# Merging K^T V stretches of two batches, moving the transfers that feed them, and splitting the last copy of an attention and MLP kernel

## The chip, the cores and the metric

The kernel runs on one core of a Trainium2 chip. The metric is the device time of one execution in microseconds (us). A profile's span is some 1.8 us shorter than the time. Executions of one kernel spread by 1 to 1.5 us around 284, and each is marked fast or slow by its time and granted TensorE clock.

## The reference

For 8 batches with 8 heads, 576 positions and 64 dimensions:

```python
kv  = np.einsum('bhsd,bhse->bhde', k, v)
out = np.einsum('bhsd,bhde->bhse', q, kv)
rms = np.sqrt(np.mean(out * out, axis=-1, keepdims=True) + 1e-06)
x   = (out / rms * g_norm)      # heads joined: 4608 rows of 512
h   = x @ w_in                  # 2048 wide
g   = np.where(h > 0, h, np.exp(np.minimum(h, 0)) - 1)
y   = g @ w_out                 # 512 wide
```

## The kernel before

The kernel works through nine groups of 512 rows: one for each batch's first 512 positions, and a ninth for the last 64 positions of all batches. Group T interleaves eight steps of the first product (w_in) of group T with pieces of the second product (w_out) of group T - 1. The attention of group T + 1 is put in between, and batch T + 2 is fetched. The parts that the change touches:

```python
def kv_single(T, kv_ps, u, ls=(0, 1)):      # 36 matmuls of 64x64 for each u
    for j in range(RK):
        for l in ls:
            for s in range(2):
                ...
                nc.tensor.matmul(kv_ps[...], lhsT=bf["k", T][...], rhs=bf["v", T][...], ...)

def fetch(b):
    if b < B:
        fetch_packed_q(b)
        packed_kv(b)
        for name in "kv":
            fetch_packed_kv(name, b)
        unpack_q(b, Q)
    ...

# in group(T, ...), at = attention(T + 1), ahead = attention(T + 2):
    for i in range(8):
        rest = mm1(T, i, ...)                # 8 matmuls of w_in, ScalarE's exp
        if at and i == 3:
            at["se"](...)                    # 32 score matmuls, need kv_sb of T + 1
        for piece in second.get(i, ()):
            mm2(T - 1, *piece)               # 8 matmuls of w_out
        ...
        rest()                               # VectorE: gT
        if at and i == 0:
            at["kv"]()                       # 72 matmuls of 64x64, one copy to kv_sb
        if at and i > 5:
            at[f"xg{i - 6}"]()               # VectorE: scaling of a half of x

# in the loop over groups:
    at["landed"]()                           # gpsimd waits until q's transpose landed
    fetch(T + 2)
    ...
    group(T, ...)
    ahead["qd"]()                            # q's transposing transfer, from SyncE
```

Of the kernel before, what the change touches and what calls it, by code (L numbers as in the profile page):

```python
# [8 lines left out]
FP32 = mybir.dt.float32  # L9
# [7 lines left out]
def kernel(  # L17
# [13 lines left out]
    nc = tc.nc  # L31
    P = 128

    B, H, S, D = q.shape
    DM = H * D
# [7 lines left out]
    NT = B + 1  # L43
# [52 lines left out]
    def fetch_packed_q(b):  # L96

        t = packed.tile([P, H, J, D], BF16, name="q_pk", tag="q")
        raw["q", b] = t
        in_ = q[b].rearrange("(h s) r d -> s h r d", s=2)[:, :, 0:G, :].rearrange(  # L100
            "s h (p j) d -> p s h (j d)", j=J
        )
        for s in range(2):
            nc.gpsimd.dma_start(  # L104
                out=t[:, 4 * s : 4 * s + 4].rearrange("p h j d -> p h (j d)"), in_=in_[:, s]
            )

    def packed_kv(b):
        for name, pool in (("k", packed), ("v", qkvp)):
            t = pool.tile([P, 4, RK, D], BF16, name=f"{name}_pk", tag=name)  # L110
            raw[name, b] = t
            bf[name, b] = t.rearrange("p h j d -> p j h d")

    def fetch_packed_kv(name, b, hs=slice(0, 4)):
        in_ = (k if name == "k" else v)[b].rearrange("h r d -> (h r d)").rearrange(
            "(h p x) -> p h x", h=4, p=P
        )
        nc.gpsimd.dma_start(  # L118
            out=raw[name, b].rearrange("p h j d -> p h (j d)")[:, hs], in_=in_[:, hs]
        )  # L120
# [3 lines left out]
    def after(ap):  # L124
        nc.gpsimd.tensor_copy(out=gate, in_=ap)  # L125

    def unpack_q(b, eng):
        t = raw.pop(("q", b))
        bf["q", b] = qkvp.tile([P, J, H, D], BF16, name="q_bf", tag="q")
        for j in range(J):  # L130
            if j == J - 1:
                after(bf["v", b][0:1, 0, 0, 0:1])
            copy_on(eng, bf["q", b][:, j], t[:, :, j])
# [12 lines left out]
    def copy_on(eng, out_, in_):  # L146
        if eng is nc.scalar:
            nc.scalar.copy(out_, in_)
        else:
            eng.tensor_copy(out=out_, in_=in_)  # L150
# [6 lines left out]
    def cast_q(b, eng):  # L157
        sv = q_tile(b)
        for j in range(J):
            copy_on(eng, bf["q", b][:, j], sv[:, j])  # L160
# [3 lines left out]
    def at_tile(dtype):  # L164
        full = ps_at.tile([P, 1024], FP32, name="at", tag="at")
        return full if dtype == FP32 else full.bitcast(BF16)

    def kv_single(T, kv_ps, u, ls=(0, 1)):
# [4 lines that stand above are left out]
                    rows = slice(s * 64, s * 64 + 64)  # L173
                    nc.tensor.matmul(  # L174
                        kv_ps[l * 64 : l * 64 + 64, s, u * 64 : u * 64 + 64],
                        lhsT=bf["k", T][rows, j, 2 * u + l, :],
                        rhs=bf["v", T][rows, j, 2 * u + l, :],
                        start=(j == 0),
                        stop=(j == RK - 1),
                    )  # L180
# [59 lines left out]
    def attention(T):  # L240
        st = {}
# [109 lines left out]
        def kv_out(us):  # L351
            nc.scalar.copy(
                kv_sb[:, T].rearrange("p (s u) e -> p s u e", s=2)[:, :, us],
                st["kv"][:, :, 0:P].rearrange("p s (u e) -> p s u e", u=2)[:, :, us],
            )

        def kv_u(u):
            def product():
                st["kv"] = at_tile(FP32).rearrange("p (s x) -> p s x", s=2)
                kv_single(T, st["kv"], u)  # L360
                kv_out(slice(u, u + 1))

            return product
# [61 lines left out]

            return turn

        pieces = {"kv": kv_all, "q": q_t, "qd": q_dma, "se": se}
        pieces["landed"] = lambda: after(st["at"])
        for h in range(2):  # L430
            pieces[f"kvu{h}"] = kv_u(h)
# [122 lines left out]
    for u in range(2):  # L554
        nc.sync.dma_start(
            out=q_raw0[:, u].rearrange("p (h x) -> p h x", h=4),
            in_=q[0, 4 * u : 4 * u + 4, 0:G, :].rearrange("h (p j) d -> p h (j d)", j=J),
# [24 lines left out]
    for s in range(2):  # L582
# [5 lines left out]
        out=g_row,  # L588
        in_=bass.AP(tensor=g_norm.tensor, offset=g_norm.offset, ap=[[1, 1], [0, 2], [1, 64]]),
# [34 lines left out]
    def turned(n):  # L624
# [7 lines left out]
        out=qT0.rearrange("p (s u) t -> p u s t", u=2)[:, 0], in_=qt_ps  # L632
# [134 lines left out]
    at, ahead = attention(1), attention(2)  # L767
    for i in range(3, 8):
        mm1(0, i, relu=i in (3, 5, 7), home={5: "m2", 6: "at"}.get(i, "m1"))()
    nc.gpsimd.tensor_copy(  # L770
        out=kv_sb[:, 0].rearrange("p (s u) e -> p u s e", s=2), in_=kv0
# [8 lines left out]
    both = ps_m1.tile([P, 2, G], FP32, name="o_ps", tag="mm1")  # L780
# [40 lines left out]

    def fetch(b):
        if b < B:
            fetch_packed_q(b)
            packed_kv(b)
            for name in "kv":
                fetch_packed_kv(name, b)
            unpack_q(b, Q)
        else:
            fetch_q(B)  # L830
            cast_q(B, Q)

    def group(T, at, lead, second, relu=()):

        for piece in lead:
            mm2(T - 1, *piece)
        if T == 2:
            for i in range(8):
                n = i // 2 - 1
                early = [at[f"sum{n}"], at[f"inv{n}"]] if i in (2, 4) else ()  # L840
                rest = mm1(T, i, relu=i in relu, between=early)
                for piece in second.get(i, ()):
                    mm2(T - 1, *piece)
                if i in (2, 4):
                    at[f"mul{n}"]()
                rest()
                if i in (2, 4):
                    at[f"xd{n}"]()
                if i == 0:
                    at["kv"]()  # L850
                if i in (1, 3):
                    at["se"]({i // 2: None})
                    at[f"sq{i // 2}"]()
                if i in (5, 6):
                    at[f"xg{i - 5}"]()
            return
        for i in range(8):
            between = [at["sq1"], at["sum0"], at["inv0"], at["sum1"]] if at and i == 4 else ()
            rest = mm1(T, i, relu=i in relu, between=between)
            if at and i == 3:  # L860
                at["se"]({0: None, 1: [ps_m2.tile([P, DM], FP32, name="se_ps", tag="mm2") for _ in range(2)]})
                at["sq0"]()
            for piece in second.get(i, ()):
                mm2(T - 1, *piece)
            if at and i == 4:
                at["inv1"]()
                for n in range(2):
                    at[f"mul{n}"]()
                    at[f"xd{n}"]()
            rest()  # L870
            if at and i == 0:
                at["kv"]()
            if at and i > 5:
                at[f"xg{i - 6}"]()

    ahead["landed"]()
    fetch(3)
    at, ahead = ahead, attention(3)
    ahead["qd"]()
    for i in range(8):  # L880
# [20 lines left out]
    for T in range(2, NT):  # L901
        at = ahead if T + 1 < NT else None
        if T + 2 < NT:
            at["landed"]()
            fetch(T + 2)
            ahead = attention(T + 2)
        if T == 2:
            lead, pieces, steps = [], [(2 + i // 4, 4 * (i % 4), 4 * (i % 4) + 4) for i in range(2, 8)], range(1, 7)
        elif T < B:
            lead, pieces, steps = halves[:1], halves[1:], (0, 1, 2, 4, 5, 6, 7)  # L910
        else:
            lead, pieces, steps = halves[:1], halves[1:], range(7)
        second = {i: [piece] for i, piece in zip(steps, pieces)}
        group(T, at, lead, second, {2: (1, 2, 4, 5), B: ()}.get(T, (4, 5)))
        if T + 2 < NT:
            ahead["qd"]()
    rows = out.rearrange("(i l s) f -> l s i f", l=2, s=S)
    pieces = [(j, slice(0, DM)) for j in range(J - 1)]
    pieces += [(J - 1, slice(0, DM // 2)), (J - 1, slice(DM // 2, DM))]
    for j, cols in pieces:  # L920
        n = cols.stop - cols.start
        ps = ps_m2.tile([P, DM], FP32, name="o_ps", tag="mm2")[:, 0:n]
        for f in range(FC):
            nc.tensor.matmul(  # L924
                ps,
                lhsT=gT[B][:, f, j * P : j * P + P],
                rhs=w_out_sb[:, f, cols],
                start=(f == 0),
                stop=(f == FC - 1),
            )  # L930
        sb = outp.tile([P, DM], FP32, name="o_last", tag="o_last", bufs=5)[:, 0:n]
        nc.scalar.copy(sb, ps)  # L932
        for l, eng in enumerate((nc.sync, nc.scalar)):
            eng.dma_start(out=rows[l, G:S, j, cols], in_=sb[l * 64 : l * 64 + 64, :])

# [29 lines left out]
```

## Time and profile before

| | before |
|---|---|
| time, median of the first 3 runs | 283.71 us (283.44 to 284.33) |
| span of the profiled run | 282.0 us |
| TensorE busy | 276.0 us, 98% |
| VectorE, ScalarE, gpsimd busy | 57%, 55%, 20% |
| one K^T V stretch in the chain | 0.71 us, and 0.10 on the matmuls behind it |
| last copy | 0.37 us |

In the chain of waits, a line is a start, a duration and what the time went to. In the timeline, square brackets give how long the engine was idle before and what ended that. The lines themselves stand in the prediction.

### The profile page before, as it was taken

To read this page: it belongs to the slowest core of one execution; us is meant where nothing else is said; L and a number is where in the kernel's file an instruction comes from. 1 tells how busy PE (TensorE), PEld (TensorE's weight loads), DVE (VectorE), ACT (ScalarE), POOL (GpSimd) and SP (SyncE) were. 2 spreads that over 40 slices of the span, in tenths; PEclk is the share of its full clock that TensorE was granted. 3 is DMA by queue.
4 is the path that set the end of the run, shared out by engine and by line. 5 is a ranking of instruction groups with operands and counts; after the bars stand their busy time and mean duration, and the time that the engine had idled before them with its cause. 6 is when DMAs were issued, how large, how long until landed. Compare 5 with 4: busy or idle time off the path is not lost.

```text
span 282.0 us, 5163 instructions
## 1 busy us (share of the span) xinstructions
PE 276.0 (98%) x2134; PEld 129.8 (46%) x2134; DVE 159.8 (57%) x232; ACT 153.8 (55%) x221; POOL 56.2 (20%) x98
## 2 busy tenths in 40 slices
PE   7899999999999999999999999999999999999994
PEld 3444544445444444444444444444444444444444
DVE  2559453888388546843693469445854586444400
ACT  2679546666487438533863377337923692333311
POOL 7854422143421341004110421012000000000000
PEclk9999999999999999999999999999999999999999
DMA  7999999697796696359935795455236123010122
GB/s 196 199 200 202 208 201 191 179 170 128 178 177 114 157 157 156 74 149 121 198 78 148 95 211 73 130 114 148 55 94 76 77 38 112 0 77 0 74 76 74
DMA packets 57579, 35.98 MB, mean 128 GB/s; under 512 B 32852, under 2 KB 55124, under 8 KB 57556
## 3 DMA queue, kind: packets, MB, share of 16 engines
q0 software_dynamic: 21808, 17.30, 41.2%
q1 hardware_dynamic: 35348, 17.83, 24.7%
q10 hardware_dynamic: 400, 0.52, 0.6%
q8 instruction: 16, 0.26, 0.4%
q14 instruction: 7, 0.06, 0.1%
HBM read 36.70 MB, written 9.44 MB: 164 GB/s over the span
## 4 chain that ended last, share of the span: by engine, by line
PE 94%; DMA 2%; ACT 1%; DVE 0%; issue 0%; POOL 0%; POOLq 0%
PE h_ps L467 42%; PE o_ps L514 39%; PE o_ps L924 5%; DMA v_pk<-in_v_dram 2%; PE at L174 2%; PE at L467 1%; PE bank L684 1%; PE at L201 1%; PE h_ps L684 1%; PE se_ps L201 1%; ACT r L669 0%; ACT r L672 0%; PE at L185 0%; ACT sq L663 0%; PE se_ps L413 0%
## 5 line engine op out<-in xcount | busy, mean ns | idle before, releaser
L467 PE MATMUL h_ps<-xT,w_in_sb 128*128 128x512 bf16 x536 | 125.7, 379 | 0.0
L514 PE MATMUL o_ps<-w_out_sb,gT 128*128 128x512 bf16 x512 | 120.5, 379 | 0.0
L479 ACT ACTIVATE elu_e<-h_ps 128x1024 bf16<-128x1024 f32 (+1 forms) x71 | 70.0, 995 | 80.1 <-PE h_ps L467 78.5
L467 PEld LDWEIGHTS <-w_in_sb 128*128 128x128 bf16 x552 | 52.5, 98 | 63.3 <-DVE xT L333 1.7
L514 PEld LDWEIGHTS <-gT 128*128 128x128 bf16 x512 | 49.4, 98 | 58.4
L490 DVE TENSOR_SCALAR elu_e<-elu_e 128x1024 bf16<-128x1024 bf16 (+1 forms) x75 | 31.9, 425 | 73.4 <-ACT elu_e L479 73.4
L498 DVE TENSOR_TENSOR gT<-elu_e,h_ps 128x1024 bf16<-128x1024 bf16 (+1 forms) x51 | 60.1, 1179 | 5.3
L527 ACT COPY o_sb<-o_ps 128x512 f32<-128x512 f32 x32 | 18.6, 586 | 15.5 <-PE o_ps L514 15.5
L218 DVE TENSOR_REDUCE ss<-sq 128x16 f32<-128x1024 bf16 x16 | 19.4, 1218 | 11.1 <-ACT sq L213 10.4
L485 ACT ACTIVATE elu_h<-h_ps 128x1024 bf16<-128x1024 f32 (+1 forms) x20 | 19.5, 990 | 0.0
L150 POOL COPY q_bf<-q_pk 128x512 bf16<-128x512 bf16 x24 | 14.4, 629 | 24.3 <-DMA q_pk<-in_q_dram 24.3
L498 DVE TENSOR_TENSOR gT<-elu_e,elu_h 128x1024 bf16<-128x1024 bf16 x20 | 14.2, 709 | 2.5 <-ACT elu_h L485 1.0
L924 PE MATMUL o_ps<-w_out_sb,gT 128*128 128x512 bf16 (+1 forms) x80 | 14.1, 337 | 0.0
L125 POOL COPY gate<-qT 1x1 bf16<-1x1 bf16 x6 | 1.1, 181 | 58.4 <-DMA qT<-q_bf 58.4
L104 POOL DMA_DIRECT2D q_pk<-in_q_dram x14 | 10.6, 758 | 4.5 <-issue 1.5
L229 DVE TENSOR_TENSOR xs<-at,ss 128x512 bf16<-128x512 f32 x16 | 10.2, 682 | 1.2 <-ACT ss L225 1.2
L924 PEld LDWEIGHTS <-gT 128*128 128x128 bf16 x80 | 7.8, 98 | 6.4 <-DVE gT L498 0.4
L213 ACT ACTIVATE sq<-at 128x1024 bf16<-128x1024 f32 x9 | 9.4, 1043 | 1.6 <-PE at L201 1.0
L118 POOL DMA_DIRECT2D k_pk<-in_k_dram x12 | 8.3, 690 | 3.9 <-DMA w_in_sb<-in_moe_w_in_dram 2.4
L118 POOL DMA_DIRECT2D v_pk<-in_v_dram x12 | 8.2, 683 | 3.2 <-DMA w_out_sb<-in_moe_w_out_dram 1.8
L932 ACT COPY o_last<-o_ps 128x512 f32<-128x512 f32 (+1 forms) x5 | 2.5, 500 | 10.8 <-PE o_ps L924 10.8
L174 PEld LDWEIGHTS <-k_pk 64*64 64x64 bf16 x576 | 6.4, 107 | 4.3 <-issue 4.0
(79 smaller groups left out, 140.7 us busy)
## 6 DMA issues: line engine op xcount, KB each, us to landing
out_dram<-o_sb SPq DMA_DIRECT2D x16, 512.0 KB, 3.3
q_pk<-in_q_dram POOLq DMA_DIRECT2D x14, 256.0 KB, 5.7
k_pk<-in_k_dram POOLq DMA_DIRECT2D x6, 576.0 KB, 8.3
v_pk<-in_v_dram POOLq DMA_DIRECT2D x6, 576.0 KB, 11.6
w_in_sb<-in_moe_w_in_dram POOLq DMA_DIRECT2D x5, 256.0 KB, 7.4
st_q<-in_q_dram SPq DMA_DIRECT2D x2, 512.0 KB, 4.7
w_out_sb<-in_moe_w_out_dram POOLq DMA_DIRECT2D x2, 512.0 KB, 13.9
w_out_sb<-in_moe_w_out_dram POOLq DMA_DIRECT2D x4, 256.0 KB, 12.0
```

What stands on the lines that cost most here:

```text
L118: nc.gpsimd.dma_start(out=raw[name, b].rearrange("p h j d -> p h (j d)")[:, hs], in_=in_[:, hs])
L150: eng.tensor_copy(out=out_, in_=in_)
L174: nc.tensor.matmul(kv_ps[l * 64 : l * 64 + 64, s, u * 64 : u * 64 + 64], lhsT=bf["k", T][rows, j, 2 * u + l, :], rhs=bf["v", T][rows, j, 2 ...
L218: nc.vector.reduce_sum(out=ss, in_=sq.rearrange("p c (h e) -> p (c h) e", h=H), axis=AX.X)
L467: nc.tensor.matmul(h_ps[a][:, cs], lhsT=w_in_sb[:, c, f * P : f * P + P], rhs=x(c, cs), start=(c == 0), stop=(c == KC - 1),)
L479: nc.scalar.activation(e[:, lo:hi, :], ps, AF.Exp)
L485: nc.scalar.activation(h[:, lo:hi, :], ps, AF.Relu)
L490: nc.vector.tensor_scalar(out=e[:, lo:hi, :], in0=e[:, lo:hi, :], scalar1=1.0, scalar2=1.0, op0=ALU.min, op1=ALU.subtract,)
L498: nc.vector.tensor_tensor(out=gT[T][:, 2 * i + lo : 2 * i + hi, :], in0=e[:, lo:hi, :], in1=h, op=ALU.add if relu else ALU.max,)
L514: nc.tensor.matmul(o_ps[T, j], lhsT=gT[T][:, f, j * P : j * P + P], rhs=w_out_sb[:, f, :], start=(f == 0), stop=(f == FC - 1),)
L527: nc.scalar.copy(o_sb[T][:, j % 2, :], o_ps.pop((T, j)))
L924: nc.tensor.matmul(ps, lhsT=gT[B][:, f, j * P : j * P + P], rhs=w_out_sb[:, f, cols], start=(f == 0), stop=(f == FC - 1),)
```

## The change

The intent is to pay the entry into and exit from 64x64 tiles twice less: K^T V of batches 4 and 5 runs as one stretch in group 3, that of 6 and 7 in group 5, each in one PSUM tile. Batches 5 and 7 are then wanted a group earlier. So q's transposing transfer is issued right behind x's, which opens the next fetch earlier, and k and v go ahead of q for these two. Last, the final 128x256 copy is divided between ScalarE and VectorE. The core of the diff (the two-line helper `kv_in` and its names are cut):

```diff
     def fetch(b):
         if b < B:
-            fetch_packed_q(b)
             packed_kv(b)
+            if b < 5 or b % 2 == 0:
+                fetch_packed_q(b)
             for name in "kv":
                 fetch_packed_kv(name, b)
+            if b >= 5 and b % 2:
+                fetch_packed_q(b)
...
                 if i in (5, 6):
                     at[f"xg{i - 5}"]()
+                if i == 5:
+                    ahead["qd"]()
             return
...
-            if at and i == 0:
-                at["kv"]()
+            if i == 2 and T % 2 and T + 2 < B:
+                both = at_tile(FP32).rearrange("p (s x) -> p s x", s=2)
+                for n, a in enumerate((at, ahead)):
+                    a["kvin"](both[:, :, n * P : n * P + P])
+                for a in (at, ahead):
+                    a["kvout"]()
...
+            if i == 5 and T + 2 < B:
+                ahead["qd"]()
...
-        if T + 2 < NT:
+        if T + 2 == B:
             ahead["qd"]()
...
-        nc.scalar.copy(sb, ps)
+        if cols.stop == DM and n < DM:
+            nc.scalar.copy(sb[:, 0 : n // 2], ps[:, 0 : n // 2])
+            nc.vector.tensor_copy(out=sb[:, n // 2 : n], in_=ps[:, n // 2 : n])
+        else:
+            nc.scalar.copy(sb, ps)
```

More of the change, by code (lines that the diff above doesn't have):

```diff
@@ L355, in kv_out, with kv_in @@
             )
+        def kv_in(home):
+            st["kv"] = home
+            for u in range(2):
+                kv_single(T, home, u)
         def kv_u(u):
@@ L426, in x_u @@
             return turn
-        pieces = {"kv": kv_all, "q": q_t, "qd": q_dma, "se": se}
+        pieces = {"kv": kv_all, "kvin": kv_in, "kvout": lambda: kv_out(slice(0, 2)), "q": q_t, "qd": q_dma, "se": se}
         pieces["landed"] = lambda: after(st["at"])
```

## The prediction

> **What bounds the kernel now.** I read the page's busy times first, then the chain that ended last, then the timeline of the engines around one K^T V stretch and of the queues that feed it.
>
> ```profile
> PE 276.0 (98%) x2134; PEld 129.8 (46%) x2134; DVE 159.8 (57%) x232; ACT 153.8 (55%) x221; POOL 56.2 (20%) x98
> ...
> PE 94%; DMA 2%; ACT 1%; DVE 0%; issue 0%; POOL 0%; POOLq 0%
> ```
>
> TensorE is busy for 276.0 of 282.0 us and makes 94% of the chain; the other engines have over 40% idle. The rest of the chain is the first load (6.10 us) and the first batch's normalization, neither of which the diff touches. So time can be won in two ways only: fewer TensorE microseconds between the first 20 us and the end, or a shorter tail after the last matmul. It can be lost wherever TensorE is made to wait. The chain around the K^T V of batch 4, and the end (start us, us, what):
>
> ```profile
> 95.31 1.73 PE o_ps L514 x8
> 97.03 0.71 PE at L174 x72
> 97.74 1.83 PE h_ps L467 x8
> 99.57 1.73 PE o_ps L514 x8
> ...
> 264.43 13.92 PE o_ps L924 x80
> 278.35 0.02 issue
> 278.37 0.37 ACT o_last L932
> ```
>
> Eight 512-column matmuls take 1.73 us everywhere (0.216 us each) except behind a 64x64 stretch, where the same eight take 1.83. One K^T V therefore costs TensorE 0.71 + 0.10 = 0.81 us. The third view is what the gpsimd queue and SyncE do about this time (start us, us, engine, line, operation, tiles, idle before and its releaser):
>
> ```profile
> 87.35 1.23 SPq L326 DMA_TRANSPOSE xT<-xs  x1
> 90.83 0.34 SPq L536 DMA_DIRECT2D out_dram<-o_sb  x1
> 91.27 2.62 SPq L256 DMA_TRANSPOSE qT<-q_bf  x1
> 95.81 0.18 POOL L125 COPY gate<-qT 1x1 bf16<-1x1 bf16 x1 [7.57 <-DMA qT<-q_bf]
> 96.27 0.87 POOL L104 DMA_DIRECT2D q_pk<-in_q_dram  x1 [0.27 <-issue]
> 99.05 0.76 POOL L118 DMA_DIRECT2D v_pk<-in_v_dram  x1
> 103.74 1.92 POOL L150 COPY q_bf<-q_pk 128x512 bf16<-128x512 bf16 x3 [3.93 <-DMA q_pk<-in_q_dram]
> 110.17 0.18 POOL L125 COPY gate<-v_pk 1x1 bf16<-1x1 bf16 x1 [4.50 <-DMA v_pk<-in_v_dram]
> ```
>
> Batch 5 is fetched only after batch 4's transposed q has landed (95.81), q before k and v, and its v is there at 110.17. TensorE does not mind: it uses them in the group after this one.
>
> **What the Trainium skill says.** "TensorEngine Tiling (Array Packing)", Key Properties: "Changing tiling mode (not just tile) drains the TensorE". The trace agrees in size: an isolated stretch of 36 64x64 matmuls in batch 1 costs 0.41 us and makes the four matmuls after it 0.97 instead of 0.86, so 0.52; 72 cost 0.81. Thus 36 more cost 0.29, and 0.81 - 2 x 0.29 = 0.23 us is fixed, whatever the number. "DMA: Bandwidth & Descriptors", Anatomy of one DMA, says that a transfer has a fixed part of about 2 us, mostly completion, beside its bytes; here the first bytes after the issue at 96.27 flow only from about 98 (6 GB/s in 96 to 98, 136 in the next two). "PSUM — Partial Sum Buffer", on bank collisions, says that ScalarE and VectorE must not read the same bank and 32-partition quadrant at once. The kernel before has no such pair side by side in its trace, so nothing here confirms it, but the new last copy is exactly that pair.
>
> **The change part by part.** First, the merged stretches. K^T V of 4, 5, 6 and 7 are four stretches now, 4 x 0.81 = 3.24 us. In two stretches of 144 matmuls each costs 0.23 + 4 x 0.29 = 1.39, so 2.78 together. All of it is on TensorE's path: minus 0.46 us. The number of matmuls and the data do not change.
>
> Second, the copies out. Two CASTs of 128x256 at 0.37 us each follow the double stretch (0.74), and the score product of the next step needs their result and their PSUM tile. Between lie the eight w_in matmuls of step 3 with 1.83 us, and ScalarE's exp and output copy of step 2 are over by then. About 1 us is left: no cost.
>
> Third, the supply. In the group of T = 3 TensorE now wants batch 5 after step 2. Step 3 starts at 104.75 in the trace of before; batch 4's stretch is no longer ahead of it, so the double stretch starts at 104.75 - 0.81 = 103.94 and batch 5's half at 104.65. With the old order (landed 110.17) TensorE would stand for 5.5 us, so the two moves of transfers have to pay for this. q's transposing transfer goes right behind x's: the issue of x's second half ends at 87.35 + 1.23 = 88.58, q_bf is complete at 88.24, so q is issued at 88.6 instead of 91.27 and lands 4.54 later as now, at 93.1. The first fetch follows 0.46 later, at 93.6, and it is k. In the trace v landed 13.9 us after the first issue (96.27 to 110.17). Of that, q's 0.52 MB took about 4.1 us (136 and 110 GB/s from 98 to 102), which now comes behind: 9.8 us, so v lands at 103.4 at the latest. The output store of 0.5 MB that shared the engines from 105.4 does not fall into the new window, which should give back up to 2 us: my estimate is 101.5 to 103.4. Slack 1.2 to 3.1 us, so no wait. For batch 7 in the group T = 5 the q transfer moves more, from 151.19 to about 145.3 (x's issues end at 145.56, the schedule is then 0.23 ahead), so k is issued at 150.3, v is there by 160.1 at the latest, and TensorE wants it at 162.7: slack 2.6. q itself comes later for 5 and 7, but its unpacked form is needed only at about 117 and 175, over 5 us after it can be ready.
>
> Fourth, x behind which q now stands. x's transfers are still issued first. The scaling of x's second half starts at 122.01 because VectorE works on gT until then, while x landed at about 119.6 (3.2 after its issue ended at 116.4): q's packets behind it have 2 us to disturb before it shows.
>
> Fifth, the last copy. ScalarE's 372 ns for 128x256 becomes 128x128 on ScalarE (a 128x128 copy from PSUM has 258 ns in this trace) and 128x128 on VectorE (289 ns for a 64x128 copy from PSUM). Side by side: 0.37 - 0.29 = 0.08 us won. But both halves lie in one bank, and if the program is ordered so that they do not collide, VectorE waits for ScalarE: 0.26 + 0.03 + 0.29 = 0.58, that is 0.21 us lost. I think the ordered form likelier, 60 to 40, which makes plus 0.09 on average.
>
> Sum: 283.71 - 0.46 + 0.09 = 283.34, so **283.3 us**.
>
> **The rivals.** (a) TensorE waits for v of batch 5. For it: this batch gains only 2.7 us by the moved transpose, and my slack has 1.2 us at its low end. Against it: it needs q's removal from the front to be worth under 3 us. A late v by 1 us would make 284.3; with nothing gained by the order of k, v and q (landing at 93.6 + 13.9 = 107.5) a wait of 2.9 us, 286.2. I give a visible wait 15%. (b) The fixed part is not a cost of the switch but of the first accumulation of each batch, and merging saves nothing: about 283.7 to 283.8. Against it: the 0.10 us on the matmuls after a stretch is the same for stretches of 36 and 72 and for score stretches, so at least 2 x 0.10 = 0.2 us should go. (c) The last copy runs side by side: 283.2. (d) VectorE or the gpsimd queue becomes a bound because copies of q move under VectorE's work. Against it: VectorE is at 57%, and the same number of copies only shifts by 3 to 5 us; at most some tenths, in one group.
>
> **Range and chances.** The runs of before spread from 283.44 to 284.33, so a median moves by some 0.3 by itself. (b) and (c) span 283.2 to 283.8, (a) has a tail to 286. Range 282.7 to 284.0. A change of 2% is 5.7 us: nothing on the gaining side has that size (all K^T V stretches of these batches together are 3.2), and on the losing side only a supply failure in both groups. Faster 0.005, same 0.985, slower 0.01.
>
> **What would show it.** Right: two stretches of 144 64x64 matmuls of 1.3 us in the chain, no VectorE or DMA share in the chain beyond the first load, TensorE busy at about 275.6, gate on qT near 93 instead of 95.81, v of batch 5 seen before 104.6. Wrong: a piece "DMA v_pk" in the middle of the chain, or idle TensorE ahead of the second half of a double stretch (a); a double stretch of over 1.55 us (b). The last copy: two 128x128 copies that overlap (c), or a VectorE copy whose idle time ends with ScalarE's. The prediction as a whole falls if the time leaves 282.7 to 284.0, most likely upwards by a wait for v.

## The result, and the profile after

The changed kernel took 284.45 us as the median of six runs. One of them was a slow run of 481.57 us (clock 0.56); the five fast ones spread from 283.81 to 284.83, with a median of 284.31. The kernel before had 283.85 in six runs. A ratio here is the mean time of one kernel's fast runs over that of the kernel before in the same rounds, so not quite the ratio of the medians quoted. It is 1.0011, with a 95% interval of 0.999 to 1.0033. Two later sets of runs gave 1.0007 and 1.0013. The change is worth nothing, or costs about 0.3 us; it was expected to win 0.4.

The first profile fell in the slow run, and a second one too (738.01 us, with matmuls of 0.83 us in place of 0.38). Each was the first of that kernel's six executions, and nothing is read from their times. A third profile is fast, with a span of 282.5 us. Its page shows busy times and the chain by engine (30 of 2134 matmul records are missing, so its busy TensorE is a little low, and its chain has false gaps of 0.05 us and short detours):

```profile
PE 272.9 (97%) x2104; PEld 129.2 (46%) x2134; DVE 160.4 (57%) x233; ACT 153.5 (54%) x221; POOL 56.0 (20%) x98
...
PE 91%; ACT 3%; DMA 2%; DVE 2%; issue 1%; POOL 0%; POOLq 0%
```

TensorE is still the bound. The chain around both double stretches and at the end:

```profile
102.25 1.73 PE o_ps L519 x8
103.98 1.33 PE at L174 x144
105.31 1.83 PE h_ps L472 x8
...
162.14 1.31 PE at L174 x144
163.45 1.83 PE h_ps L472 x8
165.28 0.34 PE at L201 x16
165.68 0.46 issue
166.14 0.35 PE se_ps L201 x12
...
278.72 0.27 ACT o_last L949
279.00 0.02 issue
279.02 0.29 DVE o_last L950
```

Each double stretch takes 1.31 to 1.33 us, with 0.10 behind it, just as worked out. But in group 5, two steps after the stretch, TensorE stands for 0.46 us in the middle of its score matmuls, and the profile knows of nothing that it waits for ("issue"). At the end the two halves of the last copy come one after the other. The gpsimd queue shows the supply of batch 5:

```profile
92.74 0.18 POOL L125 COPY gate<-qT 1x1 bf16<-1x1 bf16 x1 [5.19 <-DMA qT<-q_bf]
93.26 0.75 POOL L118 DMA_DIRECT2D k_pk<-in_k_dram  x1 [0.34 <-issue]
94.56 0.75 POOL L118 DMA_DIRECT2D v_pk<-in_v_dram  x1 [0.56 <-issue]
```

The gate opens at 92.74 (predicted 93.1). By the packet records the last bytes of v leave at 101.5, and its landing is signalled at 102.16, 1.8 us before TensorE begins the stretch. There is no wait for data.

To see where the time went I cut each profile at the first w_in matmul of groups 4, 5, 6 and 7. "Steady" runs from the first w_in matmul in the steady loop's line to the end of the last matmul, and "tail" from there to the end of the span. All numbers are us from timelines of fast profiles; names are those of the experiments below.

| kernel | starts at | until group 4 | group 4 | group 5 | group 6 | steady | tail |
|---|---|---|---|---|---|---|---|
| before | 19.68 | 102.86 | 29.14 | 29.14 | 29.14 | 258.65 | 3.62 |
| changed (again2) | 19.83 | 103.38 | 28.40 | 30.37 | 28.33 | 258.86 | 3.83 |
| one_copy | 20.00 | 103.61 | 28.56 | 30.26 | 28.32 | 259.14 | 3.61 |
| split_only | 20.16 | 102.77 | 29.14 | 29.14 | 29.14 | 258.56 | 3.83 |
| moves_only | 19.95 | 102.92 | 29.33 | 29.14 | 29.13 | 258.90 | 3.61 |
| phase64 | 20.23 | 103.47 | 28.44 | 29.74 | 28.33 | 258.36 | 3.62 |
| phase118 | 19.79 | 104.85 | 28.33 | 30.15 | 28.33 | 260.03 | 3.61 |
| early_scale | 19.79 | 103.37 | 28.30 | 30.34 | 28.30 | 258.67 | 3.60 |
| phase60 | 20.40 | 103.57 | 28.41 | 29.74 | 28.33 | 258.42 | 3.62 |
| best | 20.30 | 103.46 | 28.31 | 29.72 | 28.31 | 258.13 | 3.61 |

The start differs by half a microsecond between kernels with the same program there (before and split_only), because the first transfers do. Hence the steady part is compared, and the runs' totals beside it. In the changed kernel, groups 4 and 6 lose their single stretch (0.74 and 0.81 us less). The part before group 4 gains 0.52 (group 3 by itself 0.6) and group 5 gains 1.23, where the prediction had 0.58 each. So 0.65 us too much sit in group 5, and 0.21 us in the tail.

### The profile page after: what moved, and what is told of

Read it like the earlier page. It is cut to its first block, busy times and chain, and to the rows that moved or that the text cites. A ratio compares the mean times of both kernels' runs of the same rounds, so it can differ in the third digit from the quotient of the medians.

```text
span 479.8 us, 5136 instructions
## 1 busy us (share of the span) xinstructions
PE 467.8 (97%) x2104; PEld 175.1 (37%) x2134; DVE 162.5 (34%) x233; ACT 156.6 (33%) x221; POOL 55.4 (12%) x98
## 4 chain that ended last, share of the span: by engine, by line
PE 97%; issue 1%; DVE 1%; ACT 1%; DVEq 0%
PE h_ps L472 43%; PE o_ps L519 39%; PE o_ps L940 5%; PE at L174 1%; PE at L472 1%; PE bank L689 1%; PE bank L608 1%; PE at L201 1%; PE h_ps L689 1%; PE se_ps L201 0%; PE kv_ps L174 0%; PE at L185 0%; PE bank L627 0%; PE se_ps L418 0%; PE bank L659 0%
## 5 line engine op out<-in xcount | busy, mean ns | idle before, releaser
L472 PE MATMUL h_ps<-xT,w_in_sb 128*128 128x512 bf16 x532 | 215.5, 581 | 1.0 <-issue 0.7
L519 PE MATMUL o_ps<-w_out_sb,gT 128*128 128x512 bf16 x488 | 201.9, 582 | 4.5 <-issue 3.3
L472 PEld LDWEIGHTS <-w_in_sb 128*128 128x128 bf16 x552 | 72.0, 132 | 133.2 <-issue 131.8
L519 PEld LDWEIGHTS <-gT 128*128 128x128 bf16 x512 | 66.6, 131 | 123.9 <-issue 123.0
L940 PE MATMUL o_ps<-w_out_sb,gT 128*128 128x512 bf16 (+1 forms) x79 | 24.7, 504 | 0.1
L940 PEld LDWEIGHTS <-gT 128*128 128x128 bf16 x80 | 10.5, 132 | 14.4 <-issue 12.5
L174 PEld LDWEIGHTS <-k_pk 64*64 64x64 bf16 x576 | 8.1, 133 | 5.1 <-issue 5.0
```

The costliest lines, as they stand in the source:

```text
L174: nc.tensor.matmul(kv_ps[l * 64 : l * 64 + 64, s, u * 64 : u * 64 + 64], lhsT=bf["k", T][rows, j, 2 * u + l, :], rhs=bf["v", T][rows, j, 2 ...
L472: nc.tensor.matmul(h_ps[a][:, cs], lhsT=w_in_sb[:, c, f * P : f * P + P], rhs=x(c, cs), start=(c == 0), stop=(c == KC - 1),)
L519: nc.tensor.matmul(o_ps[T, j], lhsT=gT[T][:, f, j * P : j * P + P], rhs=w_out_sb[:, f, :], start=(f == 0), stop=(f == FC - 1),)
L940: nc.tensor.matmul(ps, lhsT=gT[B][:, f, j * P : j * P + P], rhs=w_out_sb[:, f, cols], start=(f == 0), stop=(f == FC - 1),)
```

## The experiments

Theory A is the prediction's: two switches saved, no wait for v, the copies in order. Theory B: a wait for v. Theory C: the switch costs nothing. Two theories joined after the first profiles. Theory I: TensorE's own program comes late. Theory S: VectorE's scaling of x is held up by the gpsimd queue's issues.

**again**, the changed kernel once more:

> The changed kernel once more, because its first profile fell into a run whose TensorE clock was 0.56. Theory A (prediction: the merged stretches save 0.46 us of TensorE, no wait for v, the last copy in order loses 0.21): about 0.25 us under the kernel before, two stretches of 144 matmuls of about 1.3 us, VectorE's last copy waits for ScalarE's as it did in the slow profile. Theory B (TensorE waits for v of batch 5 or 7): 0.3 to 1 us over the kernel before, idle TensorE or a DMA piece inside the chain between 100 and 170 us. Theory C (the switch has no cost that merging saves): the two stretches of 144 last 1.4 us or more each with 0.1 behind them, time equal to before plus 0.2.

Measured: 284.25 us against 284.04, ratio 1.0007 (0.9987 to 1.0028). The profile was the slow one of 738 us and told nothing, so the theories stayed undecided.

**one_copy**, the changed kernel with the old last copy:

```diff
-        if cols.stop == DM and n < DM:
-            nc.scalar.copy(sb[:, 0 : n // 2], ps[:, 0 : n // 2])
-            nc.vector.tensor_copy(out=sb[:, n // 2 : n], in_=ps[:, n // 2 : n])
-        else:
-            nc.scalar.copy(sb, ps)
+        nc.scalar.copy(sb, ps)
```

> The changed kernel with the last copy undone (ScalarE alone, 128x256). Theory A: 0.2 us less than the changed kernel, 0.46 us less than the kernel before. Theory B: 0.2 us less than the changed kernel too, but still over the kernel before. If the copy were without cost: equal to the changed kernel.

Measured: 284.48 us, ratio 1.0007 (0.9986 to 1.0029); a difference of 0.2 us is below what the runs resolve. The profile resolves it: the tail is 3.61 instead of 3.83. It was also the first fast profile with the merged stretches, and its steady part was 0.49 us *longer* than before. It has three gaps that before lacks: one after the 126th matmul of the first double stretch (about 0.24 us), one of 0.35 us after the 4th score matmul into the second tile in group 5, and a late first matmul of group 5. The first in the chain, where the 126 matmuls take 1.18 us instead of some 1.15 and the other 18 take 0.34 instead of 0.16:

```profile
104.16 1.18 PE at L174 x126
105.34 0.03 issue
105.37 0.34 PE at L174 x18
```

The first two are 510 matmuls apart. With a weight load each that is 1,020 rows of TensorE's program (a row is one instruction), and with four semaphore rows between them 1,024, four times 256. "Runtime: NRT & Kernel Launch", Instruction fetch mechanics, says that an engine's instructions come by its own DMA queue in blocks of 16 KiB, 256 instructions, with a cost that is "mostly hidden". The trace agrees on the blocks: its instruction queue q8 moved 16 packets of 16,384 bytes for 4,288 rows. A double stretch is 288 rows in 1.3 us, so it may use up a block before the next has come. That is theory I.

**split_only**, the kernel before with only the last copy split (the reverse of the diff above):

> The kernel before with nothing but the last copy split. Theory A: 0.2 us slower than before, and the two halves one after the other (0.26 and 0.29 us) in the tail. If the halves ran side by side: 0.08 us faster.

Measured: 284.11 us, ratio 1.0003 (0.9982 to 1.0024). The timeline at its end:

```profile
278.76 0.27 ACT L933 COPY o_last<-o_ps 128x128 f32<-128x128 f32 x1 [1.38 <-PE o_ps L924]
279.05 0.29 DVE L934 COPY o_last<-o_ps 128x128 f32<-128x128 f32 x1 [11.40 <-ACT o_last L933]
```

VectorE waits for ScalarE, the pair takes 0.58 us for 0.37, and the tail is 0.21 us longer, as in the changed kernel. The ordered form is shown.

**merged_no_moves**, the merged stretches with the old last copy, q's transfer at the end of the group and q fetched ahead of k and v:

```diff
             packed_kv(b)
-            if b < 5 or b % 2 == 0:
-                fetch_packed_q(b)
+            fetch_packed_q(b)
             for name in "kv":
                 fetch_packed_kv(name, b)
-            if b >= 5 and b % 2:
-                fetch_packed_q(b)
...
-                if i == 5:
-                    ahead["qd"]()
...
-            if i == 5 and T + 2 < B:
-                ahead["qd"]()
...
-        if T + 2 == B:
+        if T + 2 < NT:
             ahead["qd"]()
```

> The merged stretches with the old last copy and without the moved transfers: q's transpose at the end of the group, q fetched ahead of k and v. Theory A: TensorE waits about 5.5 us for v of batch 5 (landed at 110.2 in the profile before, wanted at 104.65) and about 8 us for batch 7 (landed at 170.75, wanted at 162.7), so 13 us slower, about 297 us. Rival: if the wait hides somewhere else, under 290.

Measured: 302.35 us, ratio 1.0638 (1.0599 to 1.0676), all runs at a mean clock of 0.971. The chain in group 3:

```profile
99.36 11.45 DMA v_pk<-in_v_dram
110.81 0.04 issue
110.85 1.18 PE at L174 x61
112.03 3.53 PE h_ps L472 x8
```

TensorE waits for v until 110.8, about 6 us, and then runs at a lower clock (0.50 granted from 110.8 to 116): the eight matmuls behind it take 3.53 us instead of 1.83. Group 5 waits until 180.0. The moved transfers are thus needed, and do what they were made for. The cost of 18.3 us was higher than my 13 because the clock's loss after each wait and the later start of the second fetch (v of batch 7 issued at 167.0 instead of 158.4) were not in it.

**moves_only**, the moved transfers with the old last copy, each batch's stretch alone at step 0:

> The moved transfers (q behind x, k and v ahead of q for 5 and 7) with the old last copy and with every batch's K^T V alone, as before. The profile of the changed kernel with one last copy showed three losses in the steady part: a stall of about 0.24 us inside the double stretch of T = 3, one of 0.35 us (0.5 with the refill) in the score stretch of T = 5, and about 0.2 us at the start of T = 5 where VectorE's scaling of x took 0.72 in place of 0.48 us beside the gpsimd queue's issues. Theory I (instruction supply: each 16 KB fetch of TensorE's program is 256 rows, and a double stretch of 288 rows eats it in 1.3 us): neither of the two stalls here, since a single stretch is 144 rows; the 0.2 at the start of T = 5 stays. Rival M (the moved transfers keep TensorE or its memory busy): the stalls are here too.

Measured: 284.25 us, ratio 1.0011 (0.9996 to 1.0027). Groups 5 and 6 take 29.14 and 29.13 as before, and the stretch of group 3 has no gap, so neither stall is there: rival M falls, and the stalls belong to the merged stretches. The moves themselves cost 0.25 us of the steady part, at the borders of groups 4 and 5, where the scaling took 0.64 and 0.68 us in place of 0.48.

**again2**, the changed kernel, gave the profile shown above:

> The changed kernel once more, not first on the chip, for a profile in the fast state. Theory I: a stall after the 126th of 144 matmuls of the first double stretch and one after the 4th score matmul into the second tile in T = 5, the same places as in the kernel with one last copy, because the rows in front are the same; last copies one after the other, 0.21 us longer. A random cause (DMA load alone): stalls elsewhere or none.

Measured: 284.32 us, ratio 1.0013 (0.9997 to 1.003). The stall in group 5 is after the same 4th score matmul as in one_copy. The one in the first double stretch is not there (1.33 us): that block's fetch began at 102.14 in this trace and at 102.99 in one_copy's, and was just in time. So theory I's place is right, and whether the first border hurts depends on less than a microsecond.

**phase64**, with more rows ahead of everything, built on one_copy:

```diff
-    idle(idle_ps, 2, FP32)
+    for _ in range(65):
+        nc.tensor.matmul(
+            idle_ps[0:32, 0:48], lhsT=zeros[:, 0:32], rhs=zeros[:, 0:48], start=True, stop=True
+        )
     idle(idle_ps, 1)
```

> The changed kernel with one last copy, and 65 tiny matmuls (32 weights, 48 columns) in place of two of the warming matmuls at the start, so that TensorE's program has 129 more rows ahead of everything that follows. Theory I: the ends of the 256-row fetches then lie 64 matmuls earlier, a fetch is asked for well ahead of or late in each double stretch and never used up within 3.5 us; both stalls are gone, the steady part (first w_in matmul of the second kind to the last matmul) is about 0.7 us shorter than with one last copy, about 258.3 us against 258.99. Rival M or a wait for landing data: the stalls stay.

**phase118** is the same with 119 matmuls of 24 columns:

> The same with 119 tiny matmuls, 237 rows more. Theory I: a fetch border falls some 8 to 10 matmuls into the first double stretch and the next one 128 matmuls later is still inside it, so TensorE stands there for about 2 us (fetch of about 3.5 us less 1.2 us of work); in T = 5 about the same 0.3 us as before. Steady part about 1.5 to 2 us longer than with one last copy. Rival M: no change against the kernel with one last copy.

Measured: in phase64 both stalls are gone. Group 5 takes 29.74 us, which is 29.14 + 0.60, and the steady part is 258.36, close to the 258.3 expected. Its time is nevertheless 285.68 us, ratio 1.0054 (1.0026 to 1.0081): four of six runs had a mean clock of 0.994 and 285.3 to 286.1 us, the two others 283.75 and 283.99. The warming matmuls at the start that I took away were probably needed in some runs: phase118 lacks them too and has two of four runs at 0.994 and 0.986, and phase60 below keeps the early ones and has none of five under 0.999. How this comes about is not shown, as both profiled runs were near the full clock. In phase118 (285.94 us, ratio 1.0081, 1.0046 to 1.0116) the chain shows in group 3:

```profile
103.94 1.29 PE at L174 x139
105.23 1.23 issue
106.46 0.25 PE at L174 x5
```

The stretch stops after its 139th matmul for 1.23 us. By my count beforehand the border was to be at about 126 + 128 - 118 = 136. The trace settles the difference: it records each float32 warming matmul as two pairs of weight load and matmul, so taking two away for 119 adds 115 matmuls, and 126 + 128 - 115 = 139. (For the same reason phase64 adds 122 rows and phase60 below 118, not 129 and 121.) In group 5 the stall has moved to the second matmul of step 4 (0.24 us).

The traces allow an exact test. Counting the rows of TensorE's program from its start (two for each weight load with its matmul, one for each semaphore or drain row), the stalls come behind row 1985 and row 3009 in one_copy, 3009 in again2 and in early_scale below, and 2241 and 3265 in phase118. Each of these numbers leaves 193 when divided by 256. So the place of the stall follows the number of rows in front, while data, transfers and the work around it are the same. Theory I is shown. Its sizes were less good: for phase118 I expected a stall of about 2 us and a steady part 1.5 to 2 us longer than one_copy's; it was 1.23 us and 0.89 us longer. The 3.5 us for a fetch in these expectations fit one_copy's group 5, where TensorE goes on 3.61 us after it passed the row 256 earlier; in phase118's group 3 this was 2.52 us. The time scale of a fetch is in the packet records of the instruction queue:

| kernel, stall | packet starts | takes | TensorE goes on | from start |
|---|---|---|---|---|
| one_copy, group 3 | 102.99 | 0.95 | 105.37 | 2.38 |
| one_copy, group 5 | 163.90 | 1.22 | 166.59 | 2.69 |
| again2, group 5 | 163.51 | 1.31 | 166.14 | 2.63 |
| phase118, group 3 | 104.11 | 0.89 | 106.46 | 2.35 |
| phase118, group 5 | 164.84 | 1.51 | 167.78 | 2.94 |

TensorE goes on 1.3 to 1.5 us after the packet has ended, every time. A single stretch of 72 matmuls is 144 rows, and in groups 3 to 6 of the kernel before, 40 large matmuls (80 rows) stand between it and the next small ones, the scores. So every block there holds at least 80 rows of large matmuls. At 0.216 us a matmul these take over 8 us (an estimate), longer than any fetch in the table, and the fetch stays hidden. That is why the kernel before shows no such stall there.

**early_scale**, the scaling of x's second half ahead of the group's last gT, on one_copy:

```diff
+            if at and i == 7:
+                at["xg1"]()
             rest()
...
-            if at and i > 5:
-                at[f"xg{i - 6}"]()
+            if at and i == 6:
+                at["xg0"]()
```

> The changed kernel with one last copy, and the scaling of x's second half put ahead of the last gT of the group in VectorE's program, where VectorE waits for ScalarE's exp anyway. Theory S (the scaling next to the gpsimd queue's issues, 0.55 to 0.72 in place of 0.48 us, delays the next group's first matmul): the scaling ends over 2 us before the group's border, TensorE's first matmul after it comes without the gap of 0.08 us and the group T = 4 takes 28.33 us (28.40 and 28.56 in the two fast profiles with the change); the stall in the score stretch of T = 5 stays, since TensorE's program is unchanged. If the border waits for something else: no change at it.

Measured: 283.92 us, ratio 0.9996 (0.998 to 1.0011). Group 4 takes 28.30 us and the gap at its border is gone; the stall in group 5 stays (0.45 us), as expected. What it removed is to be seen in the timeline of the changed kernel (again2):

```profile
150.58 0.75 POOL L118 DMA_DIRECT2D k_pk<-in_k_dram  x1 [0.34 <-issue]
...
151.00 0.55 DVE L333 TENSOR_SCALAR xT<-xT,g_col 128x1024 bf16<-128x1024 bf16 x1
...
151.61 1.41 PEld L472 LDWEIGHTS <-w_in_sb 128*128 128x128 bf16 x8 [0.41 <-DVE xT L333]
```

The same row of the kernel before, whose fetch began only at 156.17:

```profile
151.14 0.48 DVE L333 TENSOR_SCALAR xT<-xT,g_col 128x1024 bf16<-128x1024 bf16 x1
```

The gpsimd queue now issues k while VectorE scales x, and the scaling takes 0.55 us (0.72 in one_copy) in place of 0.48. The weight load of the next group waits for it. phase118 is a control: there the row at this border took 0.48 us by chance of timing, and group 4 takes 28.33 us without the edit. "SBUF — State Buffer", Who interferes with whom, says that VectorE in a 2-port mode and gpsimd share a port pair that is locked for a whole instruction. The traces agree only in part. In the ten profiles of the table the row takes 0.48 to 0.49 us beside no issue. Nine rows are longer (0.52 to 0.72), and in each of them one gpsimd issue ends and the next begins. But the row of phase118 at 152.43 has a single issue beside it almost from start to end, and takes 0.48 as well. So the longer rows go with the change from one issue to the next, and whether a lock makes them longer is not shown.

**phase60**, one_copy with 61 tiny matmuls (64 weights, 48 columns) in place of the later warming matmul, `idle(idle_ps, 1, FP32)`, so that the early warming stays:

> The changed kernel with one last copy, and 121 more rows at the start of TensorE's program (61 tiny matmuls in place of the later of the warming matmuls, so that the early warming stays; the variant with 129 rows lost 2 us in four of its six runs at a mean clock of 0.994). Theory I: fetch borders 60 matmuls earlier, no stall in either double stretch or behind it, T = 5 takes 29.72 us (29.14 + 0.58) in place of 30.26 to 30.37; steady part 258.3 to 258.4 us. If the 129 rows helped by chance: stalls as with no rows added. Time: 0.3 us under the kernel before if the start is not disturbed.

Measured: no stall, group 5 takes 29.74 us, steady part 258.42. Time 284.09 us, ratio 1.0006 (0.9992 to 1.002), all runs at a clock of 0.999 or 1.0. The steady loop begins at 20.40, later than in the other profiles, which takes the gain back; part of that may be the tiny matmuls, part the first transfers' own spread.

**best**, phase60 and early_scale together:

> Both edits together. Theory I and S: steady part 258.65 - 0.46 = 258.2 us, no gap over 0.05 us in TensorE's work between the first batch and the end, time 0.3 to 0.5 us under the kernel before; below what five rounds can tell from zero with certainty, so the profile decides about the parts and the runs about the total. Rival: the start's own spread of about 1 us (first transfers, clock) swallows it and the runs say same.

Measured: 283.82 us against 283.96, ratio 0.9995 (0.9982 to 1.0007). The chain in group 5, to be held against that of the changed kernel above:

```profile
162.59 1.31 PE at L174 x144
163.89 1.83 PE h_ps L472 x8
165.72 0.34 PE at L201 x16
166.07 0.23 PE se_ps L201 x16
```

The steady part is 258.13 us, 0.52 less than before. The runs cannot tell the total from that of the kernel before: the start at 20.30 eats most of it, and 0.14 us is inside the interval. It is the lowest steady part of all, but not a version that is shown to be faster.

## Why the prediction was right or wrong

**The bound** was right: TensorE makes over 90% of the chain before and after.

**The merged stretches** were right in themselves. The fixed part of 0.23 us was read from stretches of 36 and 72 and holds for 144: 1.31 to 1.33 us and 0.10 behind, so 1.41 to 1.43 where 1.39 was worked out. Where nothing else disturbs, group 5 grows by 0.58 to 0.60 us (0.58 was worked out), and groups 4 and 6 shrink by 0.81 to 0.84. Theory C falls. The predicted saving of 0.46 us reappears as the 0.52 of the kernel "best", as near as single profiles can tell: the steady parts of before and split_only, with one program there, differ by 0.09.

**The supply of k and v** was right for batch 5. The gate was expected at 93.1 and came at 92.74; v of batch 5 was estimated at 101.5 to 103.4, and it landed at 102.16 (again2) and 102.90 (one_copy). For batch 7 it was right in the outcome alone: v was to land by 160.1 "at the latest" and landed at 161.09 and 161.74, 1.5 us before batch 7's half of the stretch, where 2.6 us of slack were worked out. In phase64 and best it landed at 163.00 and 162.94, not 0.2 us before that half begins, so this part came close to failing. Without the moves TensorE does wait. Rival (a) did not happen.

**The last copy** went the way that was held likelier, 0.21 us lost. Averaging it with the other way to 0.09 was 0.12 too little.

**What failed** is the step "In two stretches of 144 matmuls each costs 0.23 + 4 x 0.29 = 1.39, so 2.78 together. All of it is on TensorE's path: minus 0.46 us". It counted the matmuls' time and looked for waits on data only; rivals (a) to (d) named v, the switch, the copy and VectorE. None named TensorE's instruction supply. Packing 288 rows into 1.3 us leaves a fetch of 256 rows unhidden, and group 5 lost 0.65 us to it (0.46 us idle, and 12 score matmuls in 0.35 us instead of some 0.17 behind it), more than the two switches save. In moving the stretches together, the change made the one spot where the program is consumed fastest twice as long.

**The fourth part** failed in a small thing. It asked whether q's packets disturb x's landing and found 2 us of room. The disturbance came by another road: q landing earlier moves the gpsimd queue's issues onto VectorE's scaling of x, which the next group waits for. It costs 0.07 to 0.25 us of group 4. Rival (d) came nearest, with "some tenths, in one group" at low weight, but it named the copies of q and not the issues.

The sum closes: 283.34 predicted, + 0.65 (fetch), + 0.08 (border, 28.40 against 28.31), + 0.12 (copy), is 284.19. The kernel before, too, had a median of 283.85 in the larger set, 0.14 above the 283.71 that I started from. That makes 284.33, and the fast runs' median was 284.31. That the two agree to 0.02 us is luck: the terms come from single profiles, and medians of this kernel moved between 284.25 and 284.45. So the range was too narrow at its upper side by a term that was missing, and by the spread of a median of three.

What stays open: why the executions with 0.56 of the clock and of 738 us occurred, and how much of the later start in phase60 and best is owed to the added matmuls.

## What to carry to other kernels

Very small matmuls can consume TensorE's program faster than it is fetched (here 288 rows in 1.3 us, against 2.35 to 2.94 us from the start of a fetch until TensorE went on): count rows in a stretch against 256 before joining stretches, and where two borders fall close together, move them with rows elsewhere or keep large matmuls in between. When a transfer is moved earlier, follow everything that its landing releases, here the issues of the gpsimd queue, and see what they then run beside. Splitting a copy of one PSUM bank over two engines gains nothing if the two are ordered (here it lost 0.21 us).

## What the Trainium skill lacked or had wrong

- "Runtime: NRT & Kernel Launch", Instruction fetch mechanics, calls the cost of a block border "mostly hidden". It lacks the condition: here, where 288 rows of 64x64 matmuls took 1.3 us, TensorE went on 2.35 to 2.94 us after the start of the packet with the next block, and stood for 0.24 to 1.23 us.
- "TensorEngine Tiling (Array Packing)", Key Properties, gives no figure for the drain at a change of mode. Here entry and exit cost some 0.23 us together: stretches of 36, 72 and 144 matmuls cost 0.52, 0.81 and 1.41 to 1.43 us.
- "PSUM — Partial Sum Buffer", on bank collisions, does not say what a split copy costs when it is ordered: 0.58 us for two halves of 128x128, against 0.37 for one copy of 128x256.
- "SBUF — State Buffer", Who interferes with whom, says that the engine that issues second is blocked until the first one's instruction has ended. Here a VectorE instruction of 0.48 us took 0.52 to 0.72 across the change from one gpsimd issue (0.75 us) to the next, and 0.48 beside a single issue (phase118).
- No page tells of whole executions such as the two slow ones here: one with a granted clock of 0.56 from start to end (481.57 us), and one with matmuls of 0.83 us although its records show a clock of 1.0 (738.01 us).
